# Agent attention with a soft expert layer: products of two cells in rounds 9 and 10, the first expert layer in one tile, and a new written order of the last third

## The chip, the cores and the metric

The kernel runs on one core of a Trainium2 chip, all data in 32-bit floats. The metric is the time of one execution on the device in microseconds (us); lower is better. The core has a matrix engine (PE in the profile; PEld is its weight load), a vector engine (DVE), a scalar engine (ACT), a general engine (POOL) and a queue (SP) that issues the transfers between memory and the core.

## What is computed

```python
# per batch b of 4, N = 11456 tokens, C = 128 channels, 49 agents
a2k = softmax(scale * agents @ k.T);   agent_v = a2k @ v
q2a = softmax(scale * q @ agents.T);   x = q2a @ agent_v
# over all 45824 rows of x, 32 slots, 8 experts of 4 slots each, F = 1024
logits = x @ phi
d = softmax(logits, over the rows);    slot_input = d.T @ x
for e in range(8):
    slot_out[e] = maximum(slot_input[e] @ w1[e], 0) @ w2[e]
out = softmax(logits, over the slots) @ slot_out
```

The softmax over all rows means that no output row can be written before every row has been read and the experts have run.

## The kernel before

A *cell* is 128 tokens (four streams of 32); a batch has 90 cells, all four 360. K and V come in six groups of 16 (the last of 10) cells per batch, Q the same, but the last batch's Q in seven (..., 6, 4). Two Q groups make a *round*: rounds 0 to 8 belong to batches 0 to 2, rounds 9, 10, 11 (32, 32, 22 cells) and 12 (4 cells, the group with number 24) to the last batch.

Every step is declared as an operation with its engine, what it needs, and the buffers that it takes and frees (`op`, line 212). The order in which all 1281 operations are written out is a list of names by hand, `ORDER` (line 47); each engine does its own part of that list in that order, and waits where an input isn't there. A name is a family and its numbers: `qp21.1` is the second half of `qp` of Q group 21. The families that matter here:

- K side: `kE` (line 309) multiplies weights and V into `ev`, `kA` (316) adds `ev` to the running sum `acc` on DVE; after the last group of a batch `kg`/`kh` (325 to 352) turn `acc` into `bd_m`, the matrix that takes a query's agent weights to logits.
- Q side: scores, softmax (`qt` to `qN`), transposition `qp` on PE into `tp`, copy `qc` on ACT into `pT`.
- A round: `ql` (516) makes the logits `lq`; `qM` (525), `r2`, `r4` (540), `r3` find each slot's maximum of the round (`t`, `rz`, `m_all`), where `r4` is four small matmuls, one for each band of 32 rows; `qv` copies the logits to `x_all`; then the exponentials `dt` are made on POOL and ACT (`ru`, `re`), or for rounds 10 to 12 on ACT and DVE (`rx`, `ry`); `rg` (571) multiplies `dt` and the agent weights `pt`, cell by cell, with 32 columns of weights for each, into `gp`; `rc` (580) copies `gp` to `g_all`. `dt` has two buffers.
- Behind the rounds: `nm`, `wt`, `wr`, `ws` scale the rounds' maxima against each other, `gm` and `l1` (750, 754) add up the rounds of the last batch in `gt_p` (`l1` the last of them, round 12), `l2`, `l3`, `l4` make the experts' input `si`; `f0` to `f2` scale the part of the other batches; `dE`, `d1` to `d4` are the sums of the softmax.
- The experts: `mh` (786) is the first layer, experts 0 to 3 in one tile `hp` and 4 to 7 in another, 512 columns at a time; `mr` is the maximum with zero into `hs` (DVE and ACT), `mt` transposes into `htp`, `mc` copies to `ht`, `mo` (816) is the second layer into `so_p`, 64 products of 128 columns; `ms`, `sb`, `sd` make `sob`, from which all output is multiplied.
- Output: 25 chunks (4, 4, 8, 8, then 16 cells). `cr`, `cu`, `ce` make the exponentials over the slots in `x_all`; `os`, `oe`, `or`, `om` (836 to 851) divide them by their sum (`cd`), `ot` transposes to `ct`, `oo` (859) is the product with `sob` into `pa` and `pb`, `va` (DVE) and `vb` (ACT) copy to `ot`, and `od` (879) writes 1 MB to memory. The first `oo` needs `sob`.

The expert weights are loaded once the last K and V group has been used up, because they take its memory; this is the list `ends` (line 888), with `kE23` as the last.

Of the kernel before, what the change touches and what calls it, by code (L numbers as in the profile page):

```python
# [44 lines left out]
CO_N = CO_AB + P  # L45
# [52 lines left out]
qp22.0 qp22.1 qc22 cu7 cu11 ef r49 r39 eg ce2 ce14 oe2 qv9 ql12 rg10.0 eh qp23.0 r59 ru9.1 cu13
ry10.1 rg10.1 ru9.0 qz24 om3 ei oe7 qc23 qM12 ce16 r212 os4 oe1 r412 r312 rx12 ql11 or2 qv12 qM11
r211 r411 r311 nm os8 rc10 re9.1 ce11 re9.0 rx11 dE ej wt rg9.0 rg9.1 rc9 ry11.0 ry11.1 or7 wr ws  # L100
ce10 rg11.0 rg11.1 f0 ry12.0 rc11 rg12.0 rc12 gm qv10 cu17 om2 cu12 ce12 ce13 ce17 l1 l2 ce9 f1 l3
cr24 f2 l4 os17 ce7 d1 qv11 os9 w10 mh0.0 mh0.1 mr0.0 cr21 cu24 w12 mh1.0 mh1.1 mr1.0 or1 os6 os5
cu8 mt0.0 mr0.1 mt0.1 oe4 om1 ce24 mr1.1 mt1.0 mt1.1 oe8 mc0.0 om0 ot0 mo0.0 oe5 mc0.1 mc1.0 mc1.1
# [57 lines left out]
def tile_agent_attn_soft_moe(ctx, tc, qT, kT, vL, agT, phi, w1, w2, cst, out):  # L161
# [84 lines left out]
    def k_ops(i):  # L246
# [264 lines left out]
    def r_ops(ri):  # L511
        r = rs[ri]
        grp, at, n, b = r["q"], r["at"], r["n"], r["b"]
# [66 lines left out]
        def rc():  # L580
            s_.copy(out=g_all[:, ri, :], in_=r["gp"])
# [36 lines left out]
        for j, q in enumerate(grp):  # L618
            qi = q["i"]
            if late:  # L620
                d = o("ry", (j,), "V", lambda q=q: ry(q), deps=(mb,), takes=("dt",),
                      gives=(("pt", mb),))
            else:
# [430 lines left out]
```

## Time and profile before

| | us |
|---|---|
| median of 3 runs | 285.83 |
| the three runs | 283.93, 285.83, 286.65 |
| the profiled execution | 286.32 |
| its span, from the first to the last instruction | 284.3 |

In that span PE is busy for 243.7 us (86%), DVE for 221.3 (78%), ACT for 198.6 (70%), POOL for 126.2 (44%). The transfers move 103.8 MB, 365 GB/s on average over the span. Busy shares are means over very different stages, so the stages are looked at one by one.

### The profile page before, as it was taken

The page shows a single profiled execution, that of the slowest core. Times are in us where ns is not written, and L with a number is a line of the kernel's source. Part 1 is how long each engine was busy: PE and PEld are TensorE (multiplying, and loading weights), DVE is VectorE, ACT ScalarE, POOL GpSimd, SP SyncE. Part 2 cuts the span into 40 slices and gives each one's busy share as a digit, 9 for nine tenths or more (in the row PEclk, how much of TensorE's full clock was granted, in tenths as well). Part 3 has the DMA queues.
Part 4 walks back from the last instruction along what each step waited for, and adds up shares of the span by engine and source line. Part 5 has one row for each costly group of instructions (what it writes and reads, how often), then busy time and mean ns, then how long its engine had stood idle before and what let it go on. Part 6 is the DMA issues. An engine that isn't in the chain of part 4 may idle for free.

```text
span 284.3 us, 8467 instructions
## 1 busy us (share of the span) xinstructions
PE 243.7 (86%) x3370; PEld 130.6 (46%) x3370; DVE 221.3 (78%) x431; ACT 198.6 (70%) x678; POOL 126.2 (44%) x139
## 2 busy tenths in 40 slices
PE   6959889999998999999999999997599878487920
PEld 4213646543564655356664556865437422122200
DVE  0597774699998878999989999988558998686510
ACT  2459696566997876599889888988713597657630
POOL 0034521207565341565752676795602868244100
PEclk9999999999999999999999999999759797668555
DMA  7999999999999999999999999379700299999996
GB/s 251 428 418 418 420 408 416 424 403 416 342 427 419 418 420 419 395 372 417 419 418 420 408 413 411 118 308 425 308 2 2 116 415 420 412 420 425 421 417 279
DMA packets 16454, 103.82 MB, mean 365 GB/s; under 512 B 2080, under 2 KB 2464, under 8 KB 5152
## 3 DMA queue, kind: packets, MB, share of 16 engines
q1 hardware_dynamic: 16272, 103.21, 89.0%
q8 instruction: 26, 0.43, 0.6%
q10 hardware_dynamic: 144, 0.08, 0.1%
q14 instruction: 12, 0.10, 0.1%
HBM read 79.70 MB, written 23.59 MB: 363 GB/s over the span
## 4 chain that ended last, share of the span: by engine, by line
PE 52%; DMA 28%; DVE 8%; ACT 4%; issue 3%; SPq 1%; ACTq 1%; DVEq 0%
PE ev L313 12%; PE sq L236 12%; DMA qt<-qT 10%; DMA out<-ot 10%; PE sk L236 9%; PE tp L470 6%; DMA vt<-vL 4%; DMA kt<-kT 3%; ACT ot L877 3%; PE gp L577 3%; PE lq L520 3%; PE pa L864 2%; PE hp L790 2%; DVE ct L856 1%; DVE cd L838 1%
## 5 line engine op out<-in xcount | busy, mean ns | idle before, releaser
L438 ACT ACTIVATE pt<-pt,mx 128x49 f32<-128x49 f32 x148 | 47.5, 326 | 0.1
L236 PE MATMUL sk<-kt,ag 128*32 128x512 f32 (+1 forms) x384 | 45.8, 570 | 1.6 <-DMA kt<-kT 1.4
L236 PE MATMUL sq<-qt,ag 128*32 128x512 f32 (+3 forms) x400 | 43.8, 554 | 3.8 <-DMA qt<-qT 3.6
L313 PE MATMUL ev<-vt,et 128*64 128x129 f32 x720 | 44.9, 276 | 2.1 <-DMA vt<-vL 1.4
L864 PE MATMUL pa<-ct,sob 32*128 32x512 f32 (+2 forms) x50 | 35.0, 824 | 11.5 <-DVE ct L856 8.0
L877 ACT COPY ot<-pb 128x1536 f32<-128x1536 f32 (+2 forms) x25 | 32.4, 1307 | 17.4 <-DMA out<-ot 9.9
L313 PEld LDWEIGHTS ev<-vt,et 128*64 128x64 f32 x720 | 39.3, 136 | 8.9 <-issue 6.2
L459 POOL TENSOR_TENSOR pt<-pt,rt 128x784 f32<-128x784 f32 (+3 forms) x20 | 27.1, 1355 | 34.6 <-DVE rt L455 26.5
L296 ACT ACTIVATE es<-sk,nm 128x512 f32<-128x512 f32 (+1 forms) x48 | 29.7, 652 | 10.3 <-DVE nm L287 8.2
L864 PE MATMUL pb<-ct,sob 32*128 32x512 f32 (+2 forms) x150 | 36.1, 834 | 0.0
L850 POOL TENSOR_TENSOR x_all<-x_all,cd 128x512 f32<-128x512 f32 (+2 forms) x25 | 23.6, 961 | 24.9 <-DVE cd L845 24.6
L553 POOL TENSOR_TENSOR dt<-x_all,mb 128x512 f32<-128x512 f32 (+1 forms) x20 | 24.2, 1217 | 21.5 <-DVE mb L549 17.7
L306 DVE STREAM_TRANSPOSE et<-es 128x1024 f32<-128x1024 f32 (+1 forms) x24 | 28.0, 1165 | 3.1 <-ACT es L296 3.1
L589 POOL TENSOR_TENSOR x_all<-x_all,r_all 128x512 f32<-128x512 f32 (+3 forms) x25 | 23.8, 963 | 14.1 <-DVE r_all L585 8.5
L475 ACT COPY pT<-tp 128x1024 f32<-128x1024 f32 (+3 forms) x25 | 23.0, 920 | 8.8 <-PE tp L470 8.8
L268 DVE TENSOR_REDUCE mt<-sk 128x2 f32<-128x1024 f32 (+1 forms) x24 | 27.4, 1141 | 1.8 <-PE sk L236 1.5
L438 ACT ACTIVATION_READ_ACCUMULATOR pt<-pt,mx 128x1 f32 x148 | 28.0, 189 | 0.0
L864 PEld LDWEIGHTS pa<-ct,sob 32*128 32x128 f32 x50 | 10.2, 246 | 33.7 <-DVE ct L856 22.1
L874 DVE COPY ot<-pa 128x512 f32<-128x512 f32 (+2 forms) x25 | 15.5, 624 | 12.9 <-DMA out<-ot 9.5
L413 DVE STREAM_TRANSPOSE pt<-sq 128x1024 f32<-128x1024 f32 (+3 forms) x20 | 21.9, 1097 | 2.0 <-PE sq L236 1.5
L236 PEld LDWEIGHTS sq<-qt,ag 128*32 128x32 f32 x400 | 10.9, 109 | 23.4 <-issue 16.7
L470 PE MATMUL tp<-cs,pt 128*128 128x128 f32 x140 | 21.3, 283 | 0.0
(126 smaller groups left out, 421.6 us busy)
## 6 DMA issues: line engine op xcount, KB each, us to landing
out<-ot SPq DMA_DIRECT2D x21, 1024.0 KB, 7.2
vt<-vL SPq DMA_DIRECT2D x20, 1032.0 KB, 11.1
qt<-qT SPq DMA_DIRECT2D x20, 1024.0 KB, 9.4
kt<-kT SPq DMA_DIRECT2D x19, 1024.0 KB, 9.3
w2s<-w SPq DMA_DIRECT2D x4, 1024.0 KB, 9.4
w1s<-w SPq DMA_DIRECT2D x4, 1024.0 KB, 15.1
vt<-vL SPq DMA_DIRECT2D x4, 645.0 KB, 8.3
kt<-kT SPq DMA_DIRECT2D x4, 640.0 KB, 9.1
```

Of the source, the lines that this page charges most:

```text
L236: t_.matmul(sp[32 * q4:32 * q4 + 32, h, :nt], ag[:, b, 32 * h:32 * h + 32], xv[:, q4, :], start=True, stop=True)
L268: v_.tensor_reduce(out=k["mt"][:, 0:2], in_=k["s"][:, :, :nt], axis=AX.X, op=ALU.max, negate=True)
L296: s_.activation(out=k["e"][:, h, :nt], in_=k["s"][:, h, :nt], func=AF.Exp, bias=k["nm"][:, 2 * h:2 * h + 1])
L306: v_.transpose(out=k["et"][:, :n].rearrange("p t (h a) -> p h t a", h=2), in_=k["e"][:, :, :nt].rearrange("p h (t a) -> p h t a", a=32))
L313: t_.matmul(k["ev"][o:o + AW, :], k["et"][:, c, :], k["v"][:, c, :], start=c < 2, stop=c >= n - 2)
L438: s_.activation(out=x, in_=x, func=AF.Exp, bias=q["mx"][:, c:c + 1], accum_out=q["rt"][:, c:c + 1])
L459: g_.tensor_tensor(out=x, in0=x, op=ALU.mult, in1=q["rt"][:, :n].unsqueeze(2).to_broadcast([P, n, A]))
L470: t_.transpose(q["tp"][:, h, j % 4, :], q["pt"][:, 2 * j:2 * j + 2, :].rearrange("p c a -> p (c a)"), ident)
L553: g_.tensor_tensor(out=q["dt"][:, :q["n"]], in0=x_all[:, q["at"]:q["at"] + q["n"]], op=ALU.add, in1=r["mb"].unsqueeze(1).to_broadcast([P, ...
L589: g_.tensor_tensor(out=x_all[:, x], in0=x_all[:, x], op=ALU.subtract, in1=r_all[:, x].unsqueeze(2).to_broadcast([P, q["n"], S]))
L864: t_.matmul(pb[:, r - 1, :32 * n] if r else pa[:, :32 * n], sob[32 * r:32 * r + 32, :], z["ct", j][32 * r:32 * r + 32, :32 * n], start=Tru ...
L877: s_.copy(out=o_ov(j)[:, 1:4], in_=z["pb", j][:, :, :32 * CHUNKS[j]])
```

## The change

- `rg` of rounds 9 and 10 (`PAIRS`) takes two cells in one matmul: 64 columns of weights, 100 columns of data, into a `gp` of two halves, of which only the two diagonal blocks are wanted. `rc` copies both halves to `g_two`, and `lsum` picks the blocks by masked scales `ws2` (from `sel_eo`), two matmuls for every round of the last batch.
- `r4` of the last batch's four rounds is one matmul with the full selection matrix in place of four.
- Round 12's `dt` has a buffer of its own (`dl`); round 11 (`LAST_SUM`) is added last in place of 12.
- `m_h`: the two experts j and j+4 are added into the same 32 rows of `hp`, 256 columns at a time, so that `hp`, `hs`, `htp` and `ht` hold half as many elements; each half (`fh`, `q`) has its own chain. `m_out` is 32 products of 256 columns (two experts side by side), and `sb` picks the right half with two matmuls against `sel_e`, which is made once by two ACT instructions in `am`.
- The weights `w1` and `w2` are laid out in memory to suit; the constants have 66 more columns.
- `ORDER` is new from the step behind `kA21` on (422 of its 1281 names).

```diff
@@ from kA21 on, two lines of the list
-qp21.1 qc21 cu16 qN19 cu2 cr15 kv22 ka22 qw24 kE22 cr12 kA22 kv23 qE22.3 qw22 kE23 ce4 re8.0 qr24
+qu19 qc20 qe19 kE21 kb23 kr23 qd19 ke23.0 ke23.1 kT23 qp21.0 ru8.0 qw19 ka23 w22 ka21 kA21 qp21.1
+qc21 cu16 kv22 kE22 kv23 cu11 kE23 cr14 cr17 cu7 qw24 ka22 qE22.3 ce16 qr24 qr19 ce7 cr15 qr23
...
+    "dl": 1, "s": 3, "a": 2, "oa": 2, "ob": 2, "ot": 4, "ct": 4,
+LAST_SUM = NR - 2
+PAIRS = (9, 10)
...
         def r4():
+            if b == B - 1:
+                t_.matmul(r["t"][:, 4:8], sel_d, r["z"], start=True, stop=True)
+                return
...
         def rg(j, q):
+            if ri in PAIRS:
+                if j == 0:
+                    r["gp"] = tile_("a", [P, 2, A1], f"gp_{ri}")
+                for c in range(0, q["n"], 2):
+                    o_ = 32 * (c % 4)
+                    cc = q["c0"] + c
+                    t_.matmul(r["gp"][o_:o_ + 64], q["dt"][:, c:c + 2, :].rearrange("p c s -> p (c s)"),
+                              q["pt"][:, c:c + 2, 0:A1], start=cc < 4, stop=cc >= n - 4)
+                return
...
     def am():
         s_.mul(out=ag[:, 1:], in_=ag[:, 1:], mul=SCALE)
+        for h in range(2):
+            s_.activation(out=sel_e[:, h], in_=sel_d, func=AF.Copy,
+                          scale=cs[:, CO_EM + h:CO_EM + h + 1])
...
+    def lsum(ris):
+        for ri in ris:
+            for x in range(2):
+                t_.matmul(z["gt"], g_two[:, ri - n0, x if ri in PAIRS else 0, :], ws2[:, x, ri - n0, :],
+                          start=ri == n0 and not x, stop=ri == LAST_SUM and x == 1)
...
+    def m_h(fh, q):
+        if q == 0:
+            hps[fh] = tile_("s", [P, 2, 512], f"hp_{fh}")
+            hss[fh] = tile_("pt", [P, 2, 512], f"hs_{fh}")
+        for e in range(E):
+            j = e % 4
+            t_.matmul(hps[fh][32 * j:32 * j + 32, q, :256], si[:, e, :],
+                      z["w1"][:, 2 * fh + e // 4, j, q * 256:q * 256 + 256],
+                      start=e < 4, stop=e >= 4)
...
+            v_.tensor_scalar(out=hss[fh][:, 0, :256], in0=hps[fh][:, 0, :256], scalar1=0.0,
+                             scalar2=None, op0=ALU.max)
         else:
-            s_.activation(out=hss[eh][:, 1], in_=hps[eh][:, 1], func=AF.Relu)
+            s_.activation(out=hss[fh][:, 1, :256], in_=hps[fh][:, 1, :256], func=AF.Relu)
...
+    def m_out(x):
+        if not x:
+            z["so"] = tile_("a", [P, 2, C], "so_p")
+        for i in range(2):
             for j in range(4):
+                t_.matmul(z["so"][32 * j:32 * j + 32],
+                          hts[x // 2][:, x % 2, i, 32 * j:32 * j + 32],
+                          w2s[x][:, i, 2 * j:2 * j + 2, :], start=not x + i,
+                          stop=x == 3 and i == 1)
...
     def m_sb():
         z["sb"] = tile_("a", [P, C], "sb_p")
-        t_.matmul(z["sb"], sel_d, so, start=True, stop=True)
+        for h in range(2):
+            t_.matmul(z["sb"], sel_e[:, h], so[:, h], start=not h, stop=h == 1)
```

Three places of the new order. First DVE, from the sum of the K group 21 to that of the last group 23 (`ev_21` to `ev_23`; `r_all` rows are `cr`, `rt` rows are `qr`). Before:

```order
L319 SCALAR_TENSOR_TENSOR acc_18_2291<-acc_18_2291,al_21_2692,ev_21_2650 128x129
L455 RECIPROCAL rt_19_2673<-rt_19_2673 128x16
L585 TENSOR_REDUCE r_all_65<-x_all_64 128x16 x2
L319 SCALAR_TENSOR_TENSOR acc_18_2291<-acc_18_2291,al_22_2707,ev_22_2710 128x129
L455 RECIPROCAL rt_24_2566<-rt_24_2566 128x4
L319 SCALAR_TENSOR_TENSOR acc_18_2291<-acc_18_2291,al_23_2688,ev_23_2736 128x129
```

and in the changed kernel:

```order
L326 SCALAR_TENSOR_TENSOR acc_18_2296<-acc_18_2296,al_21_2697,ev_21_2655 128x129
L607 TENSOR_REDUCE r_all_65<-x_all_64 128x16
L607 TENSOR_REDUCE r_all_65<-x_all_64 128x10
L462 RECIPROCAL rt_24_2571<-rt_24_2571 128x4
L462 RECIPROCAL rt_19_2678<-rt_19_2678 128x16
L607 TENSOR_REDUCE r_all_65<-x_all_64 128x16
L462 RECIPROCAL rt_23_2303<-rt_23_2303 128x6
L326 SCALAR_TENSOR_TENSOR acc_18_2296<-acc_18_2296,al_22_2747,ev_22_2708 128x129
L326 SCALAR_TENSOR_TENSOR acc_18_2296<-acc_18_2296,al_23_2693,ev_23_2728 128x129
```

One reduction of 10 cells and one small reciprocal more now stand ahead of the two sums, and one sum has moved behind all of them.

Second PE, from the last round's maxima (`t_11`) to the experts' input (`si_p`); `gp_9` to `gp_12` are the products of the rounds, `gt_p` their sum, `fb` is `f1`, `de_p` is `dE`. Before:

```order
L542 MATMUL t_11_3020<-rz_11_3022,cs_58 32x4 x4
L715 MATMUL de_p_3038<-cs_58,gt_107 32x1 x3
L577 MATMUL gp_9_3044<-pt_18_1852,dt_18_2987 32x50 x16
L577 MATMUL gp_9_3044<-pt_19_2557,dt_19_2966 32x50 x16
L699 MATMUL wr0_3083<-wt_105,cs_58 128x4
L577 MATMUL gp_11_3087<-pt_22_2358,dt_22_3078 32x50 x16
L577 MATMUL gp_11_3087<-pt_23_1826,dt_23_3080 32x50 x6
L577 MATMUL gp_12_3114<-pt_24_2453,dt_24_3111 32x50 x4
L710 MATMUL gt_p_3120<-wse_106,g_all_66 50x32 x4
L745 MATMUL fb_3134<-fd_111,sel_on_76 128x32
L762 MATMUL si_p_3136<-gt_107,av_72 128x32
```

and in the changed kernel:

```order
L550 MATMUL t_11_2988<-rz_11_2990,cs_58 128x4
L590 MATMUL gp_9_3006<-pt_18_1857,dt_18_2963 64x100 x8
L598 MATMUL gp_12_3015<-pt_24_2458,dt_24_2995 32x50 x4
L590 MATMUL gp_9_3006<-pt_19_2562,dt_19_2966 64x100 x8
L726 MATMUL wr0_3031<-wt_107,cs_58 128x4
L598 MATMUL gp_11_3036<-pt_22_2363,dt_22_3034 32x50 x16
L598 MATMUL gp_11_3036<-pt_23_1831,dt_23_3053 32x50 x6
L746 MATMUL gt_p_3062<-ws2_109,g_two_67 50x32 x8
L781 MATMUL fb_3078<-fd_114,sel_on_77 128x32
L798 MATMUL si_p_3085<-gt_110,av_73 128x32
L751 MATMUL de_p_3093<-cs_58,gt_110 32x1 x3
```

Round 12 has moved ahead of round 11, `de_p` behind the input, and the products of round 9 are 16 matmuls in place of 32.

Third PE again, the experts. Before, with the sixteen pairs of rows for each of `ht_0` and `ht_1` shown by their first pair:

```order
L790 MATMUL hp_0_3150<-w1s_2857,si_75 32x512 x8
L790 MATMUL hp_1_3164<-w1s_2857,si_75 32x512 x8
L806 MATMUL htp_0_3181<-cs_58,hs_0_3159 128x128 x8
L806 MATMUL htp_1_3195<-cs_58,hs_1_3173 128x128 x8
L822 MATMUL so_p_3210<-w2s0_2785,ht_0_3205 32x128 x2
L822 MATMUL so_p_3210<-w2s1_2852,ht_0_3205 32x128 x2
...
L822 MATMUL so_p_3210<-w2s2_2690,ht_1_3229 32x128 x2
L822 MATMUL so_p_3210<-w2s3_2854,ht_1_3229 32x128 x2
```

and in the changed kernel:

```order
L828 MATMUL hp_0_3098<-w1s_2859,si_76 32x256 x16
L828 MATMUL hp_1_3126<-w1s_2859,si_76 32x256 x8
L844 MATMUL htp_0_3148<-cs_58,hs_0_3099 128x128 x4
L828 MATMUL hp_1_3126<-w1s_2859,si_76 32x256 x8
L857 MATMUL so_p_3164<-w2s0_2825,ht_0_3149 32x256 x8
L844 MATMUL htp_1_3175<-cs_58,hs_1_3127 128x128 x2
L857 MATMUL so_p_3164<-w2s1_3182,ht_0_3149 32x256 x8
L844 MATMUL htp_1_3175<-cs_58,hs_1_3127 128x128 x2
L751 MATMUL d_p_3210<-cs_58,gt_110 32x1
L857 MATMUL so_p_3164<-w2s2_2695,ht_1_3176 32x256 x8
L857 MATMUL so_p_3164<-w2s3_3200,ht_1_3176 32x256 x8
```

The transposes and the second layer now stand between and behind the halves of the first layer, and there are half as many of each.

## Rows read from the trace of the kernel before

**Rows 1.** Stages, busy us of each engine (count), clock, DMA share, GB/s.

```profile
core 0: us, PE busy (x) PEld busy (x) DVE busy (x) ACT busy (x) POOL busy (x), PEclk, DMA share, GB/s
197.00:202.40 5.40, 2.82 (x138) 2.10 (x124) 3.64 (x12) 3.87 (x12) 4.88 (x7) 1.00 1.02 420
202.40:212.60 10.20, 7.75 (x65) 3.44 (x57) 5.30 (x11) 3.24 (x8) 1.41 (x2) 0.50 0.19 76
212.60:216.00 3.40, 3.40 (x33) 1.95 (x29) 2.27 (x7) 1.81 (x8) 0.76 (x2) 0.99 0.00 0
216.00:222.40 6.40, 4.91 (x148) 4.40 (x143) 6.27 (x19) 1.36 (x5) 3.38 (x4) 1.00 0.01 3
222.40:230.00 7.60, 6.23 (x48) 2.75 (x40) 7.54 (x18) 6.40 (x14) 5.76 (x6) 0.78 0.63 251
230.00:281.80 51.80, 32.59 (x148) 11.08 (x144) 30.25 (x61) 30.37 (x34) 17.81 (x18) 0.66 1.01 419
```

**Rows 2.** The chain that ended last: start us, us, what.

```profile
204.14 2.16 issue
...
207.53 0.20 DVE si L765
...
207.77 6.10 PE hp L790 x32
...
213.90 0.69 DVE hs L797
...
221.45 0.35 DVE sob L834
...
228.56 1.44 ACT ot L877
```

**Rows 3.** Timeline of PE: start us, us, what, [idle before <- releaser].

```profile
200.24 0.19 PE L715 MATMUL de_p<-cs,gt 50*32 50x1 f32 x1 [0.51 <-issue]
200.36 0.91 PE L577 MATMUL gp<-pt,dt 128*32 128x50 f32 x64
...
206.30 0.63 PE L745 MATMUL fb<-fd,sel_on 32*128 32x32 f32 x2 [2.17 <-issue]
```

**Rows 4.** Engines and DMA queues of the page; two stages, columns as rows 1.

```profile
PE 243.7 (86%) x3370; PEld 130.6 (46%) x3370; DVE 221.3 (78%) x431; ACT 198.6 (70%) x678; POOL 126.2 (44%) x139
...
q8 instruction: 26, 0.43, 0.6%
...
200.24:206.29 6.05, 3.36 (x127) 2.77 (x127) 3.22 (x9) 3.99 (x12) 3.35 (x5) 0.68 0.68 276
193.92:200.24 6.32, 4.07 (x126) 2.87 (x126) 5.28 (x15) 5.19 (x16) 4.57 (x6) 1.00 1.02 425
```

**Rows 5.** Timeline of DVE and ACT: last sums, round 11's exponentials, `l2`.

```profile
182.99 0.31 DVE L319 SCALAR_TENSOR_TENSOR acc<-acc,al,ev 128x129 f32<-128x129 f32 x1
...
183.38 1.22 DVE L585 TENSOR_REDUCE r_all<-x_all 128x16 f32<-128x512 f32 x2
...
185.00 0.35 DVE L319 SCALAR_TENSOR_TENSOR acc<-acc,al,ev 128x129 f32<-128x129 f32 x1
...
199.44 0.83 ACT L559 ACTIVATE dT<-lq,m_all 128x704 f32<-128x704 f32 x1
...
204.16 0.18 DVE L758 COPY gt<-gt_p 50x32 f32<-50x32 f32 x1 [0.18 <-PE gt_p L710]
```

**Rows 6.** Groups of instructions by form: count | busy us, mean ns | idle before.

```profile
L313 PE MATMUL ev<-vt,et 128*64 128x129 f32 x720 | 44.9, 276 | 2.1 <-DMA vt<-vL 1.4
...
L822 PE MATMUL so_p<-w2s,ht 128*32 128x128 f32 x128 | 3.7, 273 | 0.0
L874 DVE COPY ot<-pa 128x256 f32<-128x256 f32 x2 | 0.8, 387 | 0.0
L838 DVE TENSOR_REDUCE cd<-x_all 128x16 f32<-128x512 f32 x21 | 13.5, 654 | 0.0
L874 DVE COPY ot<-pa 128x512 f32<-128x512 f32 x21 | 14.3, 679 | 12.9 <-DMA out<-ot 9.5 <-PE pb L864 3.3
```

More of the change, by code (lines that the diff above doesn't have):

```diff
@@ L44 @@
 CO_AB = CO_DD + P
-CO_N = CO_AB + P
+CO_EM = CO_AB + P
+CO_EO = CO_EM + 2
+CO_N = CO_EO + 2 * S
 ORDER = """
@@ L98 @@
[L98 to L103, printed above, removed]
@@ L580, in rc @@
         def rc():
-            s_.copy(out=g_all[:, ri, :], in_=r["gp"])
+            s_.copy(out=g_two[:, r_] if ri in PAIRS else g_two[:, r_, 0] if b == B - 1 else
+                    g_all[:, ri, :], in_=r["gp"])
         def cr(q):
@@ L802, in m_trans @@
-    def m_trans(eh, fh):
-        if fh == 0:
-            htp[eh] = tile_("s", [P, 2, 4, P], f"htp_{eh}")
-        for i in range(4):
-            t_.transpose(htp[eh][:, fh, i, :], hss[eh][:, fh, i * P:(i + 1) * P], ident)
-    def m_copy(eh, fh):
-        if fh == 0:
-            hts[eh] = tile_("pt", [P, 2, 4, P], f"ht_{eh}")
-        if fh == 0:
-            s_.copy(out=hts[eh][:, 0], in_=htp[eh][:, 0])
-        else:
-            v_.tensor_copy(out=hts[eh][:, 1], in_=htp[eh][:, 1])
-    def m_out(eh, fh):
-        if not eh and not fh:
-            z["so"] = tile_("a", [P, C], "so_p")
-        for f in range(4):
+    def m_h(fh, q):
[7 more added lines that the diff above has]
+                      start=e < 4, stop=e >= 4)
@@ L820, in m_out, with m_copy @@
+    def m_copy(fh, q):
+        if q == 0:
+            s_.copy(out=hts[fh][:, 0, 0:2], in_=htp[fh][:, 0, 0:2])
+        else:
+            v_.tensor_copy(out=hts[fh][:, 1, 0:2], in_=htp[fh][:, 1, 0:2])
+    def m_out(x):
+        if not x:
+            z["so"] = tile_("a", [P, 2, C], "so_p")
+        for i in range(2):
             for j in range(4):
-                e = 4 * eh + j
-                t_.matmul(z["so"][32 * j:32 * j + 32, :], hts[eh][:, fh, f, 32 * j:32 * j + 32],
-                          w2s[e // 2][:, e % 2, 4 * fh + f, :], start=not eh + fh + f,
-                          stop=eh + fh == 2 and f == 3)
+                t_.matmul(z["so"][32 * j:32 * j + 32],
+                          hts[x // 2][:, x % 2, i, 32 * j:32 * j + 32],
+                          w2s[x][:, i, 2 * j:2 * j + 2, :], start=not x + i,
+                          stop=x == 3 and i == 1)
@@ L941, in tile_agent_attn_soft_moe @@
+    mo = None
+    for x in range(4):
+        mo = op("mo", (x,), "P", lambda x=x: m_out(x),
+                deps=[c[x // 2][x % 2], wy[x], ("am", 0)] + ([mo] if mo else []),
+                takes=() if x else ("a",), gives=(("pt", t[x // 2][0]),))
+    ms = op("ms", (), "V", m_so, deps=(mo,), gives=(("a", ("mo", 0)),))
     b0 = op("sb", (), "P", m_sb, deps=(ms,), takes=("a",))
```

150 lines of the change are left out of this document (80 added, 70 removed).

## The prediction, written before the changed kernel ran

> **What bounds the kernel now.** I read the stages first, then the chain of waits, then the timeline where the chain has a hole. The end of the program is bound by the transfers: from 230.0 to 281.8 us they run at 419 GB/s without a gap, and nothing follows but 2.5 us of landing [rows 1]. Ahead of it the transfers all but stand still: 76 GB/s from 202.4 to 212.6, then 0 and 3, and 251 GB/s from 222.4 to 230.0 [rows 1]. The output can't start before `sob`, and the loads can't run on, as everything is loaded. So what counts is how early `sob` is there (221.45 + 0.35 = 221.80 [rows 2]) and how fast the first chunks follow it (the chain meets the transfers with the ACT copy that ends at 228.56 + 1.44 = 230.0 [rows 2]). All engines have slack elsewhere; a microsecond saved between the last K group and `sob` is one off the end, as long as the stores are fed.
>
> Three things fill that hole. (1) PE stands for 2.16 us from 204.14 with nothing that it waits for ("issue") ahead of `fb` [rows 2, 3]; `fb` needs `fd` and `sie`, both long there. (2) The first layer takes 6.10 us from 207.77 [rows 2], most of it at half clock: the granted clock is 0.50 from 202.4 to 212.6 and 0.99 behind [rows 1], the 1.2 and the 2.4 GHz level. It fell when PE had worked 2.82 of 5.4 us, and rose 4.9 us after `hp` began without a pause. (3) From the first `hs` at 213.90 to `sob` the chain is almost only DVE [rows 2], which is busy for 6.27 of 6.4 us up to 222.4 [rows 1].
>
> For (1) the trace hints at the program code. The queue of kind "instruction" brings 0.43 MB in 26 packets [rows 4]; PE has 3370 + 3370 records, so one packet is about 259 of them. PE also stopped for 0.51 us in the middle of the three `de_p` matmuls, where nothing can be waited for [rows 3], and from that stop to `fb` it starts 127 + 127 records; the 6.32 us before hold 126 + 126 [rows 4]. With a few pure waits that is two pieces of one size, and each follows the one before by no less than 6.05 to 6.32 us while the loads run. PE got through the second one in 3.9 us and stood for the rest. The Trainium skill, "Runtime: NRT & Kernel Launch", section "Instruction fetch mechanics", says that code comes in blocks of 256 instructions and that crossing into a new block is mostly hidden. The size agrees with [rows 4]; "hidden" doesn't agree with the 2.16 us at this place, if I read the stop rightly. By that rule the sum would lack its term of 2.0 us.
>
> **The change part by part.**
>
> *Code count.* A product is four PE records, a transpose two. Up to `fb` the change takes out 32 products of rounds 9 and 10 (128 records), 12 of the maxima (48), moves 3 `de_p` behind (12), and adds 4 in `gt_p` (16): 172 records fewer. The border that stood right at `fb` now falls 172 later: behind `fb`, `si_p`, `de_p` (20 records) and the first layer (128 and some transposes), so in `so_p`, some 7 us further on, with the loads over. The border before it falls 84 records ahead of `fb`, inside `gp_11`; the piece that ends there begins in the logits of round 12. By the steps below PE takes some 6.3 us for that stretch, just what a piece needs (6.05 to 6.32). So the stop should vanish: it holds up everything behind `l2` by 2.0 us (204.34 to 206.30 [rows 3, 5]); bounds 0 and -2.0, with at most 0.5 of it back in `gp_11`.
>
> *From the K sums to `l2`.* On DVE two reductions of 16 cells, one of 10 and three reciprocals now stand between the sum of group 21 (done at 182.99 + 0.31) and the last two sums: 183.30 + 1.22 + 0.4 + 3 x 0.2 + 2 x 0.34 = 186.2, where it was 185.35 [rows 5]: 0.85 later. PE makes up for it, since the 26 cells of round 8 (0.91 x 26/32 = 0.74 [rows 3]) no longer stand ahead of the logits of round 10. Then ACT has three activations of a group's size ahead of round 10's exponentials, where one stood, and DVE reads round 9 out earlier; I count 0.7 for this, so that round 11's exponentials end near 200.95, not at 199.44 + 0.83 = 200.27 [rows 5]. Behind them I win it back and more, because round 12 has a buffer of its own and is done ahead of round 11: one transposition, `gp_11` and its copy, and two matmuls of `l1` are left, and the later of that and DVE's read-out of round 11 (0.9) lets `l2` end near 203.5, at 204.34 before [rows 5]: -0.8. Bounds: +0.7 (the loss alone) and -1.5 (the gain alone).
>
> *Products of two cells.* No row has 64 columns of weights with 100 of data. Now 32 cells take 0.91 us [rows 3], 0.46 a group. The nearest row, 64 columns with 129, has 720 records in 44.9 us, 62 ns each [rows 6]: 16 records of 100 columns are 0.77 us. At best the halved record count halves the time, 0.23. I take 0.77: PE works 1.2 us more on the four groups, in a stretch where it works 2.82 of 5.4 us [rows 1], and `gp_11` waits for DVE's transposes anyway; if that cover goes, the two of round 9 cost 0.6.
>
> *First layer.* Columns are the same, 32 products of 256 in place of 16 of 512, so 6.10 us if the clock rises 4.9 us after the start as before, and 0.5 for the two transposes that now stand inside it. `fb` now stands ahead of `l2`, so that only `si_p` (two records like `fb`'s 0.63 [rows 3]) and `l4` (0.20 [rows 2]) follow `l2`: 203.5 + 0.9 = 204.4, before 207.53 + 0.20 [rows 2]. The layer ends near 211.0. At half clock throughout it would be 6.8, at full 3.4.
>
> *Second layer.* 64 records of 256 columns for 128 of 128: the same columns, 3.7 us at full clock [rows 6], bounds 3.2 and (half clock) 7.4. It can start at once, since `ht_0` was made beside the first layer; with two transposes and `d_p` between it ends near 215.2. The halved `hs` and `ht` take about 0.39 (the copy of 256 columns [rows 6]) for 0.69 (`hs` [rows 2]) on DVE.
>
> *To `sob`.* DVE has 30 instructions from `l4` to `sob`; the 26 of 212.6 to 222.4 took 2.27 + 6.27 us, 0.33 each [rows 1], so it needs 9.9 us and is through at 214.4 if it never waits: no longer ahead of PE. Copy of `so_p`, two products, and a sum and a reciprocal queued ahead of `sob` on DVE are 1.5 us: `sob` near 216.75, for 221.80: -5.05 us.
>
> *Stores.* The stretch at 419 GB/s stays 51.8 us [rows 1]. Behind the first `oo` DVE has 80 instructions for 79, POOL 24 for 25, ACT two 16-cell exponentials more, and ACT does two of them ahead of the second copy. I take 0.5 us off the gain for a slower ramp: -4.5. Bounds 0 and -2 of the gain.
>
> *At no cost.* The two copies of `sel_e` (ACT, early, far from the chain; 0.6 us if they weren't) and 66 more columns of constants (34 KB, 0.08 us at 419 GB/s). `w1` is loaded ahead of two pieces of `w2`; SP waits for the same `kE23`, the loads end near 204 as before (420 GB/s up to 202.4 [rows 1]), and `so_p` asks for the last ones from 211 on; if one were late, `so_p` alone would wait. One matmul for four in the maxima changes only the count. The four more in `gt_p` run beside DVE's read-out; uncovered they are 0.4.
>
> **Sum.** The profiled execution took 286.32 us, 0.5 above the median of 285.83. -0.8 (`l2`), -2.0 (stop), -0.5 (`fb` no longer between `l2` and `l4`), -1.7 (experts to `sob`: 12.35 us for 14.05), +0.5 (ramp) = -4.5: 281.8 against that execution, 281.3 against the median, which I forecast. A measurement tells about 1% (2.9 us) from no change.
>
> **The rivals.**
> 1. *The clock comes back sooner or doesn't fall.* The new piece of order keeps PE busier between 197 and 202. The first layer would take 3.4 to 5 us, but DVE's 9.9 us then decide (214.4): 279.3. Against: the last exponentials are just as late, and PE still waits for them.
> 2. *The stop isn't code, or moves into `gp_11` at its full length.* Then the two counts of rows 4 agree by chance and PE stands somewhere else, or the piece that ends in `gp_11` comes late by as much. For it: the worked-out stretch is within 0.3 us of what a piece needs. 281.3 + 2.2 = 283.5. (It is also what the quoted section of the Trainium skill would lead to.)
> 3. *The clock stays at 1.2 GHz through both layers*, because transposes that wait for `hs` now break up the first layer. Then first layer 7.4, second 7.4 and transposes: +4.6, 285.8. For it: a clock of 0.66 in the stores, where PE works in pieces [rows 1].
> 4. *Stores starve (slower).* A chunk of which nothing is prepared costs DVE a sum 0.65, a copy 0.68 [rows 6], a transposition of the same size as much, a maximum of the size of the sum (0.65) and a reciprocal 0.2: 2.9 us, and a store of 1 MB takes 2.5 at 419 GB/s. Starting 5 us sooner, the stores have 5 us less preparation behind them. If 0.4 us is lost on each of the first 13 chunks, the gain is gone; with POOL's strict order behind it, 287. Against: the count of instructions left behind the first `oo` is the same, so that the same is prepared, and the transfers show no gap today.
>
> **Chances.** The forecast 0.52, rival 1 0.12, rival 2 0.14 (0.06 still over 1% faster), rival 3 0.10 (nearly all within 1%), rival 4 0.12 (half of it slower, half a lost gain within 1%). Faster by over 1%: 0.52 + 0.12 + 0.06 = 0.70; within 1%: 0.08 + 0.09 + 0.06 = 0.23; slower: 0.06 + 0.01 = 0.07. The range reaches from rival 1 (279.3) past rival 2 nearly to rival 3: 279.2 to 285.2; slower, most of rival 3 and a little below are left out.
>
> **What would show it.** Right: no "issue" of over 0.7 us on PE between the maxima of round 11 and `hp`; `hp` starts at 204 to 205 us; the clock rises some 5 us later; `so_p` follows within 1 us of the last `hp`; `sob` at 216 to 218; 419 GB/s from about 225.5 on. Wrong: a stop of 2 us at `gp_11` or `fb` (rival 2), clock 0.50 beyond 213 (rival 3), transfers under 400 GB/s behind 226 (rival 4), or a last `acc` later than 187, which would move everything behind it.

## The result, and the profile after

| | before | changed |
|---|---|---|
| median (17 runs each) | 286.26 us | 283.25 us |
| lowest, highest | 283.93, 288.13 | 281.86, 286.60 |
| profiled execution, its span | 286.32, 284.3 | 284.20, 282.3 |

The ratio is 0.9896 (95% interval 0.9874 to 0.9918): 3.0 us or 1.04% faster, where 4.5 us were forecast; by the interval the gain is 0.8 to 1.3%. Ratios leave out executions over 1.5% above the fastest of their kernel, among them one of the changed kernel's 17, one of x1's four, two of x4's four, three of x7's ten and one of x12's twelve. The stages of the changed kernel, cut where its clock or its transfers change:

```profile
core 0: us, PE busy (x) PEld busy (x) DVE busy (x) ACT busy (x) POOL busy (x), PEclk, DMA share, GB/s
199.40:202.90 3.50, 3.50 (x42) 2.90 (x42) 1.78 (x6) 1.37 (x4) 2.61 (x4) 0.51 1.01 417
202.90:205.69 2.79, 2.71 (x73) 2.37 (x73) 2.34 (x8) 2.13 (x8) 0.00 (x0) 1.00 0.69 282
205.69:212.60 6.91, 5.67 (x85) 2.85 (x86) 5.32 (x17) 3.22 (x11) 2.98 (x4) 1.00 0.02 5
222.40:230.00 7.60, 5.66 (x37) 2.01 (x40) 6.77 (x15) 6.11 (x9) 5.65 (x7) 1.00 0.90 365
226.00:228.00 2.00, 1.38 (x13) 0.45 (x8) 2.00 (x7) 1.85 (x4) 0.24 (x1) 1.00 1.05 430
230.00:232.00 2.00, 2.00 (x8) 0.50 (x4) 1.77 (x4) 0.41 (x3) 0.28 (x1) 0.53 0.94 385
230.00:237.00 7.00, 6.90 (x24) 2.27 (x20) 6.72 (x16) 4.73 (x7) 2.33 (x3) 0.51 0.95 392
237.00:279.80 42.80, 24.88 (x115) 8.74 (x111) 22.32 (x42) 23.77 (x27) 12.63 (x13) 0.70 1.00 415
```

Two things stand out. The clock is at half for 3.5 us only and back at 202.9, ahead of the experts; before, it came back at 212.6. And the transfers reach 430 GB/s from 226, about as soon as forecast, but don't hold it: from 230 to 237 they run at 392, where before they ran at 419 from 230 on [rows 1]. What holds them back there was not tested. PE's timeline, and the page's counts:

```profile
195.08 1.59 PE L590 MATMUL gp<-pt,dt 128*64 128x100 f32 x32
...
199.31 1.55 PE L590 MATMUL gp<-pt,dt 128*64 128x100 f32 x16
200.79 0.40 PE L598 MATMUL gp<-pt,dt 128*32 128x50 f32 x8
201.12 1.60 PE L590 MATMUL gp<-pt,dt 128*64 128x100 f32 x16
...
204.58 0.40 PE L781 MATMUL fb<-fd,sel_on 32*128 32x32 f32 x2
...
205.69 2.80 PE L828 MATMUL hp<-w1s,si 128*32 128x256 f32 x48
```

```profile
PE 244.4 (87%) x3252; PEld 131.4 (47%) x3252; DVE 220.6 (78%) x431; ACT 198.7 (70%) x680; POOL 126.3 (45%) x139
```

`fb` follows without the 2.17 us of issue of [rows 3], and PE has 118 + 118 records (matmul + weight load) fewer than in [rows 4]. The chain that ended last, from the first layer on (start us, us, what):

```profile
205.69 1.98 PE hp L828 x32
207.69 0.42 DVE hs L834
...
208.53 1.16 DVE cd L875 x2
209.69 0.33 DVE hs L834
210.02 0.59 DVE r_all L607
...
211.46 1.07 PE so_p L857 x16
...
214.30 0.43 DVE ht L850
214.76 0.38 ACT ht L848
...
215.18 1.93 PE so_p L857 x32
...
218.49 0.35 DVE sob L871
...
221.74 3.07 POOL x_all L887 x3
```

PE at full speed now waits for the others: from the first `hs` to the second layer (211.46), and again ahead of its last part (214.30 to 215.18), the path is DVE's and ACT's, with sums of output chunks (`cd`) and maxima (`r_all`) standing in the queue ahead of `hs` and `ht`. Cut into three stages, with the experiments below (from the profiled executions; "end" is the end of the span):

| run | first logits of round 10 to `hp` | `hp` to `sob` done | first store to end | ratio to before |
|---|---|---|---|---|
| before | 19.18 | 14.03 | 61.3 | 1 |
| changed | 17.40 | 13.15 | 62.3 | 0.9896 |
| x6, before with borders shifted | 17.93 | 14.44 | 62.1 | 1.0089 (late start) |
| x7, pairs in round 9 only | 16.72 | 13.15 | 62.3 | 0.9899 |
| x8, no pairs | 18.29 | 14.86 | 62.1 | 1.0031 |
| x13, pause of PE | 19.45 | 14.86 | 62.4 | 1.0073 |
| x5, experts' order | 15.96 | 11.24 | 64.9 | 0.9881 |
| x11, hand-offs only | 17.35 | 11.58 | 62.6 | 0.9818 |

### The profile page after: what moved, and what is told of

Read it like the earlier page. It is cut to its first block, busy times and chain, and to the rows that moved or that the text cites. A ratio compares the mean times of both kernels' runs of the same rounds, so it can differ in the third digit from the quotient of the medians.

```text
span 282.3 us, 8243 instructions
## 1 busy us (share of the span) xinstructions
PE 244.4 (87%) x3252; PEld 131.4 (47%) x3252; DVE 220.6 (78%) x431; ACT 198.7 (70%) x680; POOL 126.3 (45%) x139
## 4 chain that ended last, share of the span: by engine, by line
PE 46%; DMA 32%; DVE 9%; ACT 4%; issue 2%; POOL 2%; SPq 1%; ACTq 0%; DVEq 0%
DMA out<-ot 11%; PE sq L243 11%; PE sk L243 9%; DMA vt<-vL 9%; PE ev L320 8%; DMA kt<-kT 7%; DMA qt<-qT 6%; PE tp L477 5%; PE lq L528 4%; ACT ot L914 3%; PE gp L598 2%; DVE cd L875 2%; PE gp L590 2%; POOL x_all L887 1%; PE so_p L857 1%
## 5 line engine op out<-in xcount | busy, mean ns | idle before, releaser
L901 PE MATMUL pa<-ct,sob 32*128 32x512 f32 (+2 forms) x50 | 32.1, 750 | 12.1 <-DVE ct L893 10.1
L901 PE MATMUL pb<-ct,sob 32*128 32x512 f32 (+2 forms) x150 | 33.6, 772 | 0.1
L901 PEld LDWEIGHTS pa<-ct,sob 32*128 32x128 f32 x50 | 9.3, 226 | 31.9 <-DVE ct L893 20.2
```

What stands on the lines that cost most here:

```text
L901: t_.matmul(pb[:, r - 1, :32 * n] if r else pa[:, :32 * n], sob[32 * r:32 * r + 32, :], z["ct", j][32 * r:32 * r + 32, :32 * n], start=Tru ...
```

## The experiments

### Is the stop ahead of `fb` the code?

Theory: PE's code comes in pieces of 256 records, and while the loads run a piece follows the one before it by no less than some 6.1 us; where PE is quicker it stands. Rival: the stop belongs to `fb`.

**x1**, the kernel before with 21 small products more:

```diff
         for _ in range(WARM):
             t_.matmul(w, ...)
+        for _ in range(21):
+            t_.matmul(w[:, 0:4], si[:, 0:4].rearrange("p e x -> p (e x)"),
+                      si[:, 0, 0:4], start=True, stop=True)
```

> The kernel before with 21 more small products (4 columns) in the warm-up at the start, which nobody reads: 84 more PE records ahead of everything, so that each border between two pieces of 256 code records falls 84 records earlier, and nothing else changes. Theory (code supply is a rate: border to border takes at least some 6.1 us while the loads run at 420 GB/s): the stops of 0.51 us in the de products and of 2.16 us at the broadcast fb vanish; the borders now fall in the products of rounds 8 or 9 (near 196.3) and of round 11 (near 202), where PE stops for about 1.3 and 0.8 us with nothing to wait for. The sum is 2.1 for 2.7 us, so that the time moves little: ratio to before 0.994 to 1.002. Rival (the stop belongs to fb, not to the code): fb still starts some 2.2 us after the sums gt_p and there is no new stop; ratio 0.998 to 1.002.

The small products took 5.85 us and everything started that much later, so the ratio (1.022, 1.0138 to 1.0302) says nothing. The trace does:

```profile
210.40 0.56 PE L577 MATMUL gp<-pt,dt 128*32 128x50 f32 x18 [0.33 <-DVE dt L565]
212.06 1.38 PE L577 MATMUL gp<-pt,dt 128*32 128x50 f32 x34 [1.10 <-issue]
213.36 0.90 PE L713 MATMUL gt_p<-wse,g_all 128*50 128x32 f32 x8
214.19 0.63 PE L748 MATMUL fb<-fd,sel_on 32*128 32x32 f32 x2
```

`fb` follows `gt_p` at once, and PE stands in the middle of round 11's products, after 18 of their 44 PE records. That is where the shifted border is counted to lie: 84 records ahead of `fb` are 16 of `gt_p`, 16 of round 12 and 52 of round 11's 88, which leaves 36, or 18 + 18. The row names nothing that PE waits for. The stop in `de_p` is gone too; the one expected near 196.3 didn't come.

**x3** (`PAIRS = ()`, 32 such products ahead) and **x4** (`PAIRS = (10,)`, 48) change the code and keep the last border in round 11.

> The changed kernel with the products of rounds 9 and 10 one cell at a time again: 128 PE records more, and 128 in the warm-up, so that the border that lies in round 11's products stays there. Theory 1 (pairs are slow at half clock, 1.55 us a group): round 9's two groups take 0.9 each, and the sum l2 comes up to 1.2 us sooner; without any stop the ratio to before would be 0.985 to 0.987 (0.990 for the changed kernel). Theory 2 (code supply is a rate): the border ahead of the last falls inside round 10's products, 3.6 us after the one before it, and PE stops there for up to 2.4 us with nothing to wait for; with both the ratio is 0.989 to 0.996. Rival to both: pairs and code don't bind, ratio 0.990 as the changed kernel.

> The changed kernel with only round 10's products in pairs, round 9's one cell at a time: 64 PE records more, and 192 in the warm-up, which keep the border in round 11's products. Theory (pairs at half clock cost 0.65 us a group more than single cells; code supply 6.1 us from border to border): 1.2 us are saved in round 9, and a stop of up to 0.8 us appears inside round 10's products, 5.3 us after the border before; ratio to before 0.986 to 0.990. Rival (DVE's transposes of round 11, not PE, set the sum l2): l2 stays at 204.7 and the ratio at 0.990.

Both started 11 and 17 us late (ratios 1.0472, 1.0392 to 1.0553, and 1.055, 1.046 to 1.064), so that their times answer nothing. Of x3:

```profile
208.11 0.82 PE L598 MATMUL gp<-pt,dt 128*32 128x50 f32 x55
210.65 0.30 PE L598 MATMUL gp<-pt,dt 128*32 128x50 f32 x9 [1.72 <-issue]
...
215.97 0.71 PE L598 MATMUL gp<-pt,dt 128*32 128x50 f32 x18
217.60 0.83 PE L598 MATMUL gp<-pt,dt 128*32 128x50 f32 x26 [0.92 <-issue]
```

and of x4:

```profile
210.71 1.24 PE L590 MATMUL gp<-pt,dt 128*64 128x100 f32 x23
213.42 0.59 PE L590 MATMUL gp<-pt,dt 128*64 128x100 f32 x9 [1.47 <-issue]
```

PE stood 55 and 23 PE records into round 10's products, and in both runs again 18 into round 11's (in x4 for 1.26 us). From the end of one stop to the end of the next PE starts 127 + 127 records in x3 as in x4, the size of a piece in [rows 4], and it takes 6.95 and 6.96 us, where it was 6.05 to 6.32. The theory holds; its figure is a lower bound. (The queue of [rows 4] brings 27 packets in x1, x3, x4 and x6, whose PE has 3380 to 3412 records of each kind, and 26 in the runs with up to 3370.)

**x6** gives the kernel before the same shift at no late start, as was meant: 26 products of 32 columns of weights and 4 of data in place of the five of the warm-up (`t_.matmul(w[0:32, 0:4], si[:, 0], si[:, 0, 0:4], ...)`).

> The kernel before with the five products of the warm-up replaced by 26 small ones (32 columns of weights, 4 of data), which together should take no longer: the same 84 more PE records and the same borders as in the run with the shifted borders, without its late start. Theory (code supply): no stop at fb, a stop of 0.3 to 1.1 us in round 11's products after 18 PE records, where that run had 1.10 us; hp starts some 1 to 2 us sooner than 207.77; ratio to before 0.993 to 0.998, as the ramp of the stores takes part of it. Rival (a stop of PE there is worth nothing, since the start of the stores is bound otherwise): ratio 0.998 to 1.002.

Missed: 1.0089 (1.0055 to 1.0122). The small products took 2.93 us for 4.01, but the first scores behind them 3.64 for 1.92, so that round 10's first logits were 3.6 us late. What follows them is nevertheless comparable: the stop is behind the same 18th PE record (1.24 us), and from these logits to `hp` it takes 17.93 us for 19.18. So, with one trace of each, the phase of the borders alone is worth 1.25 us of the 2.7 that PE stood before; the rest needs fewer records.

### What are the pairs worth?

**x7** is the changed kernel with `PAIRS = (9,)`, **x8** with `PAIRS = ()`, nothing else.

> The changed kernel with round 10's products one cell at a time, round 9's in pairs, no other edit. 64 more PE records behind the logits of round 12, so that the border of round 11's products moves into the second group of round 9. Theory (PE is busy without a pause from 185 to 198.5, so that pairs in round 10 lie on the path): round 10's products take 0.82 us for 1.59, the logits of round 11 start 0.77 us sooner; at the new border, 6 us behind the one before, a stop of 0.2 to 1.1 us. l2 between 203.8 and 204.9; ratio to before 0.986 to 0.991. Rival (pairs save time): l2 later than 205, ratio over 0.991.

x7: 0.9899 (0.9848 to 0.9950), not to be told from the changed kernel. In the profiled execution round 10's single products take 0.91 us for 1.59 and `hp` comes 0.68 us closer to round 10's logits: pairs of cells are slower than single cells, as I had taken. No stop shows at the new border; round 9 ran at half clock there (1.60 us a group). The border isn't free, though. The ten executions fall into five of 282.4 to 283.7 us, with a mean granted clock of 0.925 to 0.939 (the profiled one among them), and five of 285.8 to 287.7 us, with 0.916 to 0.919. What may part them is seen in x12.

> The changed kernel with rounds 9 and 10 one cell at a time, no other edit: 128 more PE records behind the logits of round 12. Theory (code supply is a rate: pairs are worth their records, not their time): the border falls 29 or 30 PE records into the first group of round 9, some 4 us behind the one before, and PE stops there for 2 to 3 us; the products themselves are 0.8 us (round 10) and up to 1.3 us (round 9, at half clock) quicker; l2 between 204.5 and 206; ratio to before 0.989 to 0.995. Rival (code costs nothing there): no stop, l2 at 202.6 to 203, ratio 0.983 to 0.986.

```profile
198.25 0.55 PE L598 MATMUL gp<-pt,dt 128*32 128x50 f32 x29
200.58 0.90 PE L598 MATMUL gp<-pt,dt 128*32 128x50 f32 x43 [1.78 <-issue]
...
206.16 5.27 PE L828 MATMUL hp<-w1s,si 128*32 128x256 f32 x48
```

The stop came at the 29th record, as counted, and `l2` in the range (204.92). But the ratio is 1.0031 (1.0006 to 1.0056), not under 0.995: the first layer took 5.27 us for 48 records, 2.80 in the changed kernel. After the stop the clock stayed at half to 211.3:

```profile
201.00:206.16 5.16, 5.16 (x96) 4.64 (x84) 3.18 (x9) 2.61 (x10) 0.43 (x1) 0.50 0.68 278
206.16:211.30 5.14, 5.14 (x50) 2.29 (x48) 2.86 (x10) 1.19 (x4) 2.98 (x4) 0.51 0.01 3
```

So the pairs, with 128 PE records fewer, are worth 1.35% (0.9896 for 1.0031), although the products are slower. Theory now: a stop costs twice, its length and the clock behind it.

**x13** tests that without code. The changed kernel, with the step that round 9's second group waits for moved behind another:

```diff
-... ru9.1 cu14 r312 rx12 ql11 os1 eh ei qM11 r211 r411 w12 re9.1 ry12.0 ...
-... wt rg9.1 rc9 wr ...
+... ru9.1 cu14 r312 rx12 ql11 os1 eh ei qM11 r211 r411 w12 ry12.0 ...
+... wt re9.1 rg9.1 rc9 wr ...
```

> The changed kernel with one step moved: ACT's exponentials of round 9's second group come behind those of round 11, not ahead of them, so that PE waits some 1 to 1.7 us ahead of that group's products, where the run without pairs had its stop; the code and its borders stay. Theory (a pause of PE at this place costs twice: its length, and the clock, which then stays at half through the first layer, as it did to about 211 us in the run without pairs): the first layer's 64 records take 5 to 7 us for 3.66, sob at 220.5 or later, ratio to before 0.998 to 1.005. Rival (the pause costs its own length only, the clock recovers at 203 to 205): sob at 219.5 to 220.3, ratio 0.992 to 0.996.

```profile
202.46 1.60 PE L589 MATMUL gp<-pt,dt 128*64 128x100 f32 x16 [1.05 <-ACT dt L580]
...
208.70 4.52 PE L827 MATMUL hp<-w1s,si 128*32 128x256 f32 x48
```

```profile
202.30:208.70 6.40, 6.24 (x88) 5.66 (x89) 2.62 (x8) 2.37 (x9) 0.67 (x1) 0.50 0.55 225
208.70:212.40 3.70, 3.70 (x38) 1.77 (x40) 1.43 (x5) 0.22 (x1) 2.46 (x4) 0.52 0.00 0
```

Confirmed in the trace, and the time is beyond the range: 1.0073 (1.0032 to 1.0114). At a pause of 1.05 us the clock goes to half and stays there to 212.4; against the changed kernel `hp` is 2.05 us and `sob` 3.76 us farther from round 10's logits. This takes back the whole gain of the change.

### What binds from the experts to the stores?

**x5** reorders the steps between `l4` and `sob`. It also moves four of DVE's chunk steps behind `sob` (`cr18`, `cr19`, `cr22`, `os16`; the expectation doesn't name `cr19`), with three of POOL's and one of ACT's, and five other steps ahead of it:

```diff
-mr0.0 om1 cu12 ot1 qv12 w13 mh1.0 os12 os5 mr1.0 cr18 ej mr0.1 ... mt0.0 mt0.1 mc0.1
-mh1.1 mc0.0 mo0 ...
+... mh0.0 mh0.1 om1 ot0 os4 oe2 w13 mh1.0 mh1.1 dE mr0.0 mr0.1 ...
+... mr1.0 mt0.0 mr1.1 mt0.1 oe5 ej mc0.0 mc0.1 w21 mt1.0 mt1.1 mc1.0 mc1.1 ... mo0 ...
```

> The changed kernel with another order of the steps between l4 and sob only: all four parts of the first layer back to back on PE, then the four transpositions, then the second layer; the copy qv12 at once behind l4; the reading steps of DVE and ACT (mr, mc) ahead of the sums and maxima of the chunks that stood before them; three steps of DVE (cr18, cr22, os16 with what follows them) behind sob. Theory (hand-offs to DVE and ACT, not PE's clock, make the 13.15 us from the start of hp to sob): sob at 215.5 to 216.5 for 218.84, and with half of it lost in the ramp of the stores the ratio to before falls from 0.990 to 0.983 to 0.987. Rival (the stores' start is bound by POOL's and DVE's preparation, whatever sob does): sob sooner, but the transfers reach 419 GB/s no sooner than at 240 us, ratio 0.989 to 0.992.

`sob` is done at 214.58. The ratio, 0.9881 (0.9816 to 0.9946), lies between the two ranges and its interval covers both, but the transfers decide for the rival. From the first store at 215.79 the transfers ran so:

```profile
215.79:224.00 8.21, 6.91 (x41) 3.19 (x42) 8.21 (x19) 6.24 (x12) 4.11 (x4) 0.79 0.51 201
224.00:232.00 8.00, 6.21 (x24) 1.52 (x23) 6.66 (x16) 4.71 (x8) 4.63 (x6) 0.86 0.93 381
232.00:240.00 8.00, 6.21 (x31) 2.81 (x28) 7.07 (x16) 6.21 (x9) 4.05 (x5) 0.71 0.95 394
```

DVE was busy without a gap up to 224: first store to end is 64.9 us for 62.3. (In this run round 9's pairs ran at full clock, 0.91 us a group, on code that is the same up to there: the half clock of the changed kernel's profile isn't there in every execution.)

```profile
198.40 0.91 PE L589 MATMUL gp<-pt,dt 128*64 128x100 f32 x16
...
202.34 0.18 DVE L793 COPY gt<-gt_p 50x32 f32<-50x32 f32 x1 [0.37 <-PE gt_p L745]
```

**x9** and **x10** take DVE's sums of chunks 4 to 24 down to 2 slots, with x5's order and with the changed kernel's own:

```diff
-        v_.tensor_reduce(out=z["cd", j], in_=x_all[:, C0[j]:C0[j] + CHUNKS[j]], axis=AX.X,
+        v_.tensor_reduce(out=z["cd", j], in_=x_all[:, C0[j]:C0[j] + CHUNKS[j], 0:2 if j > 3 else S],
```

> The changed kernel with the other order of the experts' steps (as in that run) and DVE's sums of the output chunks 4 to 24 over 2 slots of 32 only: it leaves out most of the softmax denominators' sum, some 0.5 us of DVE for each of 21 chunks. With that order sob came 4 us sooner and the transfers lost it again behind 216 us (281 and 365 GB/s where 419 are possible), DVE busy all the while. Theory (DVE's preparation bounds the ramp of the stores): the transfers run at over 410 GB/s from 224 on and the time falls by 2.5 to 4 us more: ratio to before 0.973 to 0.980. Rival (POOL's products and maxima, or ACT's copies, bound it): ratio 0.985 to 0.989, as without the short sums.

> The changed kernel in its own order with DVE's sums of the output chunks 4 to 24 over 2 slots of 32 only; it leaves out most of the softmax denominators' sum. sob stays where the hand-offs put it, near 218.8, where the run with the other order and short sums had it at 215.5. Theory (what binds is the preparation of the chunks, on DVE, POOL and ACT in turn, and no longer sob): the time falls as much as there, ratio to before 0.981 to 0.986. Rival (sob binds as soon as DVE is relieved): ratio 0.987 to 0.990.

x9 gave 0.9836 (0.9806 to 0.9866), a smaller gain than the theory's 0.973 to 0.980, and its transfers were still at 388 GB/s from 224 to 232; x10 gave 0.9837 (0.9783 to 0.9891), its `sob` done at 217.44, x9's at 215.46. `sob` 2 us apart, the same time: with these orders what binds the ramp is the preparation of chunks. But with 0.5 us less of DVE on each of 21 chunks only some 1.3 us (0.9881 to 0.9836) and 1.7 us (0.9896 to 0.9837) are won, and in both pairs the intervals overlap, so that even these gains aren't clear of noise. DVE is one of several; in x9's chain POOL's subtraction of the maxima and ACT's copies follow.

**x11** moves nothing behind `sob`; it only takes the needless waits away:

```diff
-mr0.0 om1 cu12 ot1 qv12 w13 mh1.0 os12 os5 mr1.0 cr18 ej mr0.1 ce8 ce12 oe2 om3 mt0.0 mt0.1 mc0.1
-mh1.1 mc0.0 mo0 ...
+mr0.0 om1 cu12 qv12 ot1 w13 mh1.0 mh1.1 mr0.1 os12 mr1.0 mt0.0 mt0.1 mr1.1 ce8 os5 cr18 ej om3 mc0.0 mc0.1 mt1.0 mt1.1 mc1.0 mc1.1
+oe12 oe2 oe5 ce12 ce15 w21 mo0 ...
```

> The changed kernel with a smaller edit of the order between l4 and sob: the four parts of the first layer back to back on PE, each reading step ahead of what it waited behind for no need (mr1.0 ahead of a chunk's sum, the ACT copy mc0.0 ahead of DVE's mc0.1 on the same tile, mr1.1 and mt1.1 early); nothing is moved behind sob, and behind it the order stays. Theory (the hand-offs cost 2 to 3 us, and the other order gained nothing because it moved DVE's preparation behind sob): sob 2 to 3 us sooner than 218.84 with the same chunks prepared; ratio to before 0.981 to 0.986. Rival (preparation of the chunks, not sob, sets when the transfers run full): ratio 0.987 to 0.991, as with the changed kernel.

```profile
205.01 3.66 PE L827 MATMUL hp<-w1s,si 128*32 128x256 f32 x64
...
210.42 1.93 PE L856 MATMUL so_p<-w2s,ht 128*32 128x256 f32 x32 [0.34 <-ACT ht L847]
```

0.9818 (0.9771 to 0.9864), 281.45 us: the fastest kernel of this study that computes the whole output, and the interval lies below that of the change (not below x5's). `hp` to `sob` is 11.58 us for 13.15, and first store to end 62.6, nearly as in the changed kernel.

**x12** is x11 with `PAIRS = (9,)`.

> The same smaller edit of the order, and round 10's products one cell at a time (0.91 us for 1.59 in the trace, the logits of round 11 0.66 us sooner, no stop at the new border). Theory: 0.6 us on top of the run without it, ratio 0.979 to 0.985. Rival (preparation sets it): 0.987 to 0.991.

0.9894 (0.9858 to 0.9930): nothing on top, rather a loss of 0.8%, though the two intervals still touch. Its profiled execution was the slowest of twelve (286.13 us); it shows the stop that the expectation had ruled out:

```profile
200.14 0.47 PE L589 MATMUL gp<-pt,dt 128*64 128x100 f32 x5
201.43 1.26 PE L589 MATMUL gp<-pt,dt 128*64 128x100 f32 x11 [0.81 <-issue]
...
207.32 5.74 PE L827 MATMUL hp<-w1s,si 128*32 128x256 f32 x64
```

Here round 9 ran at full clock up to the border, 5 PE records into its second group, and PE stood there, with half clock through the first layer behind it. The times of the twelve executions suggest how often that happens: seven took 281.6 to 282.7 us, with a mean granted clock of 0.931 to 0.936, and five 283.9 to 286.1 us, with 0.918 to 0.920. That the stop is what parts them is argued, not shown, as only one was traced. Even the seven, with a median of 282.15 us, are not below x11's 281.45, so that the 0.6 us forecast is not seen without the stop either.

The change has more parts than the pairs. The first and second layer with half the elements, round 12's own buffer and the new order were not taken back one at a time, so that what each is worth is not shown.

## Why the prediction was right, and where not

Time and verdict lie in the forecast: 283.25 in 279.2 to 285.2, faster by 1.04%, though the interval reaches below 1%. The forecast of -4.5 was too large by 1.5. The time alone is that of rival 2 (283.5) and not of the forecast (281.3). The trace decides against rival 2: PE's rows name no issue from round 11's maxima to `hp`. Of the other signs named beforehand, `so_p` followed the last `hp` within 0.4 us, but `hp` started at 205.69, not 204 to 205, the clock was up before that and not 5 us behind it, and `sob` was late. Up to round 11's exponentials the times were near the forecast (last sum of the K side done at 186.43 for 186.2, the exponentials done at 200.47 for 200.95). From there, point by point, on the two profiled executions:

- **Code stop (-2.0) and `fb` (-0.5): right.** From `l2` done to `hp` it is 0.82 us (204.87 to 205.69) for 3.43, -2.6. In the experiments eight stops of 0.81 to 1.78 us, in six runs, lie at counted borders. The rule of the Trainium skill ("Runtime: NRT & Kernel Launch", section "Instruction fetch mechanics") agrees in its blocks of 256. That a crossing is mostly hidden holds for the number of crossings: before, with 26 packets, PE's rows name an issue of over 0.3 us only three times (0.66, 0.51 and 2.17 us). It didn't hold at these borders, where PE would have been through the piece in less than some 6 us.
- **`l2` (-0.8): wrong, it came 0.5 us later** (204.87, forecast 203.5). The failed step is the price of the paired products, "16 records of 100 columns are 0.77 us": that is what round 10's took at full clock (1.59 for two groups), but round 9's ran at half, 1.55 and 1.60, on PE's path to `gp_11`, and the transposes of round 11 waited for them (idle 0.62 and 1.08 us, below). The price of 0.6 for a lost cover was too small for the same reason. x5, the same code up to `l4`, bears this out: with round 9 at full clock `l2` is done 15.14 us behind round 10's first logits (187.38 to 202.52), where it was 15.75 before and 16.58 in the changed kernel.
- **Experts to `sob` (-1.7): -0.9, and for another reason.** The step that failed is "6.10 us if the clock rises 4.9 us after the start": the clock was back before the start, as rival 1 had it, and PE's 64 records of the first layer took 3.87. (In x8 and x13, with a pause of PE of 1.78 and 1.05 us ahead, it stayed at half to 211.3 and 212.4; in the changed kernel PE ran on from 199.0.) The sentence "DVE needs 9.9 us and is through at 214.4 if it never waits" hid the loss: DVE waits for PE, PE for DVE's `hs` behind two sums, ACT for DVE's half of the same tile. `sob` was done at 218.84, not 216.75. That two errors, a first layer 2.2 us too dear and hand-offs at no cost, partly offset each other is luck. x11 took 1.6 us of it back without making anything faster.
- **Ramp (+0.5): +1.0.** First store to end 62.3 us for 61.3, with 392 GB/s from 230 to 237, which was rival 4's sign (under 400 behind 226). x5 shows rival 4's mechanism: against round 10's logits `sob` came 3.4 us sooner than in the changed kernel, and 2.6 were given back (64.9 for 62.3).

Sum: -2.6 + 0.5 - 0.9 + 1.0 = -2.0, the difference of the two spans (284.3 to 282.3). The medians differ by 3.0, as the profiled execution of the changed kernel lies 0.95 above its median. DVE's rows up to `l2`:

```profile
200.98 0.71 DVE L577 STREAM_TRANSPOSE dt<-dT 128x512 f32<-128x512 f32 x1 [0.62 <-PE gp L590]
202.77 0.38 DVE L577 STREAM_TRANSPOSE dt<-dT 128x192 f32<-128x192 f32 x1 [1.08 <-PE gp L590]
...
204.69 0.18 DVE L794 COPY gt<-gt_p 50x32 f32<-50x32 f32 x1 [0.30 <-PE gt_p L746]
```

What the forecast had missed altogether is that a stop can cost more than its length. In x8, where one of 1.78 us came back, the clock stayed down behind it, and nothing of the gain was left. That the stop before cost as much again through the clock is not shown.

## What to carry to other kernels

Count an engine's instructions as a resource: where PE runs through 256 records faster than code arrives (here some 6 us, with the loads at over 400 GB/s), fewer records can win even when each is slower. The places of the borders can be counted beforehand, though not every border costs a stop. A short pause of PE ahead of a matmul stage is paid twice where the granted clock falls behind it, so fill it or move it. And a stage made sooner pays only as far as what it feeds is prepared: take needless waits out of the hand-offs (the reading steps first in each queue, one tile's halves in the order in which they become ready) before moving work behind the stage.

## What was not expected of the hardware

- The granted clock was 0.50 (1.2 GHz) from 202.4 to 212.6 before, where PE had worked 2.82 of the 5.4 us ahead [rows 1], and from 201.0 to 211.3 in x8 and 202.3 to 212.4 in x13, where PE had paused for 1.78 and 1.05 us. In x8 it stayed so though PE was then busy without a gap. In the changed kernel it was so from 199.4 to 202.9 only, behind a pause of 0.47 us, and in x5, behind one of 0.48, not at all. What brings it back isn't settled.
- A product of two cells (64 columns of weights, 100 of data) costs 0.099 us of PE at full clock (1.59 / 16; 0.114 in x5's round 9, 0.91 / 8) where two single cells cost 0.057 (0.91 / 16).
- A product of 4 columns on 128 columns of weights is not small: 21 of them took 5.85 us at the start of x1, 0.28 each on average, with the granted clock at 1.00 up to 9 us and at 0.50 from 10 us on; 26 with 32 columns of weights took 2.93 us in x6, 0.11 each, at 1.00.
